# Moving the o tiles of batches 4 to 7 one slot later in a linear-attention plus MLP kernel

## Chip, cores and metric

One NeuronCore of one Trainium2 chip at a time. The metric is device time in microseconds (us), lower is better. The kernel before takes 292.99 us, the median of three runs (292.66 to 293.11). The experiments were run in three sets, each on another chip and each with the kernel before in it; ratios are taken within a set. A profile is one execution; its span is about 1.8 us shorter than the timed run.

## The reference, cut to what matters

Eight batches, eight heads, 576 rows, head width 64. Attention without a softmax, an RMS norm per head, then a residual MLP of width 512 → 2048 → 512.

```python
kv  = einsum('bhsd,bhse->bhde', k, v)          # 64 x 64 per head
out = einsum('bhsd,bhde->bhse', q, kv)         # called o below
x   = out / rms(out) * g_norm                  # 512 wide: 8 heads side by side
xn  = (x - mean(x)) / std(x) * g_ln
y   = x + relu(xn @ w_ch1) @ w_ch2
```

## The kernel before

The MLP is the bulk of the work: per batch 64 matmuls of 128x512 in `mm1` (the centred x, times `w1`) and 64 in `mm2` (times `w2`). The attention part of a batch is threaded into the MLP of earlier batches. The author does it by hand: `mm1` and `mm2` call `tick()` before every four such matmuls, and each tick is a slot, in which the work that `at(slot, ...)` put there is emitted. A slot lasts four matmuls. Batch `b` has its `mm1` in slots 32b to 32b+15 and its `mm2` in 32b+16 to 32b+31 (for b from 3 up).

```python
    def turn_q_dma(b):                  # q copied to another layout, then transposed by DMA
        q_p = kv_in.tile([128, JJ, H, D], bf16, tag="qp", bufs=2)
        nc.vector.tensor_copy(q_p.rearrange("p j h d -> p h j d"), q_in[b % NB])
        q_t = qt_pool.tile([128, JJ, HP, 128], bf16, tag="qt", name="qt")
        nc.sync.dma_start_transpose(
            q_t.rearrange("p j hp t -> p (j hp) t"), q_p.rearrange("p j h d -> p (j h d)"))
        qts[b] = q_t
    # [...]
    def plan_tile(s, make, turn_at, on_pe):
        # [...]
        def first():                    # o matmuls (PE), square (ScalarE), reduction (VectorE)
            t = make(); box.append(t); t.o(); t.sq(); t.red()
        def second():                   # 1/rms, times g_norm, centred (VectorE)
            t = box[0]; t.y(); t.x(); t.xc()
        # third: variance (ScalarE); fourth: xc transposed to xT, by DMA or on PE
        at(s, first)
        at(s + 2, second)
        at(s + 6, third)
        at(turn_at, fourth)
    # [...]
    for b in range(3, B):
        s = 32 * b
        at(47 if b == 3 else s - 60,
           lambda b=b: load_batch(b, qts[b - 1][:1, J, HP - 1, 127:]))
        d = -41 if b == 3 else -45
        at(s + d, lambda b=b: kv_of(b))
        at(s + d + 1.7, lambda b=b: turn_q_dma(b))
        for j in range(J):              # J = 4 main tiles of 128 rows
            o = s + d + (10 if b == 3 else 12) + 5 * j
            plan_tile(o, lambda b=b, j=j: main_tile(b, j), o + 6, False)
        if b % 2:                       # one remainder tile for two batches, 64 rows of each
            plan_tile(s - 14, lambda b=b: rem_tile(b), s - 8, False)
        at(s + 14, lambda b=b: rstd_of(b))
```

`turn_q_dma(b)` and `plan_tile` meet at `qt`: the o matmuls of batch b load it as their stationary operand. The second argument of `load_batch` is a gate: the loads of batch b start when `qt` of batch b-1 has landed. All DMA transposes and, but for half of those of the very last tile, all output transfers are issued by SyncE, in the order in which they are emitted.

Of the kernel before, what the change touches and what calls it, by code (L numbers as in the profile page):

```python
# [14 lines left out]
def kernel(  # L15
# [80 lines left out]
    def load_batch(b, after=None):  # L96
        if after is not None:
            nc.gpsimd.tensor_copy(gate, after)  # L98
        load(k_in[b % NB], k, b)
        load(v_in[b % NB], v, b)  # L100
        load(q_in[b % NB], q, b)
# [97 lines left out]
    def turn_q_dma(b):  # L199
# [6 lines that stand above are left out]
# [22 lines left out]
    def kv_of(b):  # L228
        kv_ps = ps_m.tile([128, HP, D], f32, tag="misc", name="kv_ps")
        kvp = held[b] = kv_pack[b % 4]  # L230
        for hp in range(HP):
            for j in range(JJ):
                for hh in range(2):
                    h = 2 * hp + hh
                    nc.tensor.matmul(kv_ps[hh * D:hh * D + D, hp, :],  # L235
                                     lhsT=k_in[b % NB][:, h, j, :], rhs=v_in[b % NB][:, h, j, :],
                                     start=(j == 0), stop=(j == JJ - 1))
        nc.scalar.copy(kvp[:D, :, :D], kv_ps[:D])  # L238
        nc.scalar.copy(kvp[D:, :, D:], kv_ps[D:])
# [104 lines left out]
    def main_tile(b, j, pool=None, tag="ops"):  # L344
        q_t, kvp = qts[b], held[b]
        if b not in blks:
            blks[b] = new_block("main", 3)
        return Tile([(slice(0, 128), lambda hp: q_t[:, j, hp, :], kvp)], blks[b], j, pool, tag)

    def rem_tile(b):  # L350
        mms = []
        for half, bb in enumerate((b - 1, b)):
            qt, kp = qts.pop(bb), held.pop(bb)
            mms.append((slice(half * 64, (half + 1) * 64),
                        lambda hp, qt=qt: qt[:, J, hp, :64], kp))
        if "rem" not in blks:
            blks["rem"] = new_block("rem", 1)
        return Tile(mms, blks["rem"], b // 2)

    def plan_tile(s, make, turn_at, on_pe):  # L360
        box = []

        def first():
            t = make()
            box.append(t)
            t.o()
            t.sq()
            t.red()

        def second():  # L370
            t = box[0]
            t.y()
            t.x()
            t.xc()

        def third():
            box[0].var()

        def fourth():
            box[0].turn(on_pe)  # L380
# [5 lines that stand above are left out]
# [22 lines left out]
    def rstd_of(b):  # L408
        rstd = work.tile([128, 4], f32, tag="rstd", bufs=3, name="rstd")
        nc.scalar.activation(rstd, blks[b][1][:, 2, :], func=AF.Sqrt, scale=1.0 / Dm, bias=eps_sb)  # L410
        nc.vector.reciprocal(rstd, rstd)  # L411
        rstds[b] = rstd
# [45 lines left out]
    def at(slot, fn):  # L458
        agenda.setdefault(int(slot), []).append((slot, fn))
# [153 lines left out]
# [5 lines that stand above are left out]
        at(s + d, lambda b=b: kv_of(b))  # L618
        at(s + d + 1.7, lambda b=b: turn_q_dma(b))
        for j in range(J):  # L620
            o = s + d + (10 if b == 3 else 12) + 5 * j
            plan_tile(o, lambda b=b, j=j: main_tile(b, j), o + 6, False)
        if b % 2:
            plan_tile(s - 14, lambda b=b: rem_tile(b), s - 8, False)
        at(s + 14, lambda b=b: rstd_of(b))
# [58 lines left out]
```

## Time and profile before

| | before |
|---|---|
| time, median of 3 | 292.99 us |
| PE busy | 97% of the span |
| waits of PE after 110 us, as PE's own row shows them | none |
| weight loads of o waiting for `qt` | 2.0 us in 4 waits |

In the views PE is TensorE, PEld its weight loads, DVE VectorE, ACT ScalarE, POOL GpSimd and SPq SyncE's queue. First the page's lines of busy time (us, share of the span, number of instructions):

```profile
span 291.4 us, 5801 instructions
PE 283.4 (97%) x2320; PEld 159.1 (55%) x2320; DVE 150.7 (52%) x335; ACT 154.7 (53%) x341; POOL 41.9 (14%) x68
```

PE is the limit, but 97% alone would not say whether matmuls run at their pace or stand waiting inside a "busy" record. The chain of waits says more. This is the chain of the kernel before around batch 5 (start in us, duration in us, what); L418 is `mm2`, L402 is `mm1`, L235 is kv and L260 is o:

```profile
131.81 0.75 PE kv_ps L235 x40
132.57 4.34 PE p L418 x20
136.91 6.20 DMA qt<-q_p
143.11 0.05 issue
143.16 0.40 PE o_ps L260 x4
143.56 0.86 PE p L418 x4
144.42 3.45 PE p L402 x16
147.87 0.22 PE o_ps L260 x4
```

Four matmuls take 0.86 us, 0.216 us each. The page "TensorE: Matmul & The Clock Gate" of the Trainium skill (section "Wait — 56ns, not 53.3ns?") gives 215.7 ns from start to start for 512 columns at full clock; the trace agrees, so these matmuls run at the pace that the page gives. The o matmuls at 143.16 take 0.40 us, those at 147.87 take 0.22. The first set waited for the `qt` transpose, which SyncE issued at 136.91 and which landed at 143.11. PE's own wait table does not list it, because the last matmuls before it are still counted as busy; the weight loads (PEld), which run ahead, show it. Their waits between 100 and 240 us:

```profile
PEld L260 <- DMA qt<-q_p: 2.0, 4, 0.6
```

For batches 4, 5, 6 and 7 the four stretches from the start of kv to the start of the `mm1` that follows hold exactly the same matmuls before and after the change (40 of kv, 52 of `mm2`, four of o). The columns are the stretch, its length, the busy time of PE, PEld, VectorE, ScalarE and GpSimd (with the number of instructions), the granted clock, the busy share of the DMA engines and their GB/s:

```profile
102.18:114.74 12.56, 12.47 (x97) 5.99 (x98) 7.56 (x17) 3.15 (x8) 0.85 (x2) 1.00 0.48 96
131.81:144.42 12.61, 12.49 (x98) 5.96 (x98) 4.42 (x9) 2.14 (x5) 0.85 (x3) 1.00 0.71 126
161.94:174.25 12.31, 12.31 (x98) 6.00 (x98) 7.01 (x14) 3.15 (x8) 0.86 (x3) 1.00 0.58 117
191.32:203.78 12.46, 12.46 (x97) 5.98 (x98) 4.41 (x9) 2.14 (x5) 0.00 (x0) 1.00 0.73 122
```

They differ by up to 0.30 us, though they hold the same work. (The 97 or 98 counted on PE are these 96 and the one or two that overlap an edge of the stretch.) The difference is put down to the wait for `qt`.

Why `qt` is late shows in SyncE's queue before the q transpose of batch 5 (start, time on the queue, line, operation):

```profile
135.51 1.29 SPq L341 DMA_TRANSPOSE xT_blk<-xc  x1
136.91 3.09 SPq L203 DMA_TRANSPOSE qt<-q_p  x1
```

The copy of q was done at 135.06 by VectorE's timeline, but the transpose of `xT` for tile 3 of batch 4 stood in front. Batch 7 is like this. In batches 4 and 6 VectorE was late instead: there the remainder tile's normalisation (from 105.08 and 164.55 us) precedes the copy of q, which ended at 108.43 and 167.92, and `qt` went out right after it, at 108.50 and 168.06.

### The profile page before, as it was taken

The numbers are of one execution on the slowest core, as the hardware profiler recorded it, in microseconds if no ns is written. First come the engines' busy times: TensorE is split into PE (matmuls) and PEld (weight loads), VectorE is DVE, ScalarE is ACT, GpSimd is POOL, SyncE is SP. The second block draws the span as 40 slices with busy tenths as digits, with TensorE's granted clock in tenths as the row PEclk, the third lists the DMA queues.
The fourth block names the chain that finished last, engine by engine and source line by source line (L and its number), as shares of the span: only waits on it lengthen the run. The fifth ranks groups of instructions, "written<-read, shape, count | busy, mean of one in ns | idle before, by whom it ended". The sixth has DMA issues, their size and how long they took to land.

```text
span 291.4 us, 5801 instructions
## 1 busy us (share of the span) xinstructions
PE 283.4 (97%) x2320; PEld 159.1 (55%) x2320; DVE 150.7 (52%) x335; ACT 154.7 (53%) x341; POOL 41.9 (14%) x68
## 2 busy tenths in 40 slices
PE   8889999999999999999999999999999999999995
PEld 3579755995578654444444444444444444444444
DVE  5776028836996893765266936752678200220022
ACT  3457755885569931882189408920894066016500
POOL 8522520032050003200220023000000000000000
PEclk9999999999999999999999999999999999999999
DMA  7999999469789818993999279939202510131033
GB/s 212 202 206 205 198 204 217 102 100 192 144 141 201 110 41 153 217 162 65 159 192 140 56 145 192 165 64 167 58 18 55 109 36 0 38 78 30 0 74 72
DMA packets 63290, 35.84 MB, mean 123 GB/s; under 512 B 30748, under 2 KB 58268, under 8 KB 63264
## 3 DMA queue, kind: packets, MB, share of 16 engines
q0 software_dynamic: 28016, 17.76, 43.8%
q1 hardware_dynamic: 34736, 16.99, 29.7%
q10 hardware_dynamic: 512, 0.72, 0.8%
q8 instruction: 18, 0.29, 0.4%
q14 instruction: 8, 0.07, 0.1%
HBM read 36.71 MB, written 9.44 MB: 158 GB/s over the span
## 4 chain that ended last, share of the span: by engine, by line
PE 83%; DMA 6%; DVE 6%; ACT 2%; issue 1%; POOL 1%; POOLq 0%
PE p L402 40%; PE p L418 36%; DMA qt<-q_p 4%; PE o_ps L260 3%; DMA q_in<-in_q_dram 2%; PE kv_ps L235 2%; DVE ss L287 1%; DVE x_blk L311 1%; DVE y L292 1%; DVE o_sb L423 1%; PE tp L183 1%; ACT m L405 1%; PE p L196 1%; ACT xT_blk L339 1%; PE tp L337 0%
## 5 line engine op out<-in xcount | busy, mean ns | idle before, releaser
L402 PE MATMUL p<-xT_blk,w_sb 128*128 128x128 bf16 (+2 forms) x1024 | 132.0, 286 | 0.5 <-ACT m L405 0.3
L418 PE MATMUL p<-w_sb,m 128*128 128x512 bf16 (+2 forms) x608 | 130.2, 368 | 0.0
L405 ACT ACTIVATE m<-p 128x512 bf16<-128x512 f32 x144 | 85.2, 597 | 45.3 <-PE p L402 43.5
L402 PEld LDWEIGHTS <-w_sb 128*128 128x128 bf16 x1024 | 78.6, 98 | 45.5 <-issue 1.1
L418 PEld LDWEIGHTS <-m 128*128 128x128 bf16 x608 | 56.6, 98 | 60.3
L423 DVE SCALAR_TENSOR_TENSOR o_sb<-p,rstd,x_blk 128x512 f32<-128x512 f32 (+2 forms) x38 | 27.3, 719 | 44.2 <-PE p L418 41.5
L266 ACT ACTIVATE sq<-o_ps 128x512 f32<-128x512 f32 x34 | 20.2, 595 | 38.9 <-PE o_ps L260 38.9
L287 DVE TENSOR_REDUCE ss<-sq 128x8 f32<-128x512 f32 x34 | 23.2, 682 | 19.8 <-ACT sq L266 19.8
L329 ACT ACTIVATE dev<-x_blk,st_blk 128x512 f32<-128x512 f32 x36 | 25.8, 718 | 6.2 <-DVE st_blk L315 6.1
L321 DVE SCALAR_TENSOR_TENSOR xc<-x_blk,st_blk,g_ln_sb 128x512 bf16<-128x512 f32 x34 | 25.6, 752 | 1.2
L292 DVE TENSOR_TENSOR y<-o_ps,inv 128x512 f32<-128x512 f32 x34 | 23.5, 691 | 2.6
L311 DVE SCALAR_TENSOR_TENSOR x_blk<-y,g_norm_sb 128x512 f32<-128x512 f32 x34 | 23.5, 691 | 1.2
L411 DVE RECIPROCAL rstd<-rstd 128x4 f32<-128x4 f32 x9 | 1.6, 174 | 39.3 <-ACT rstd L410 39.3
L304 DVE RECIPROCAL inv<-rms 128x8 f32<-128x8 f32 x36 | 7.2, 200 | 22.5 <-ACT rms L297 22.4
L98 POOL COPY gate<-qt 1x1 bf16<-1x1 bf16 x5 | 1.4, 287 | 115.3 <-DMA qt<-q_p 115.3
L297 ACT ACTIVATE rms<-ss,eps_sb 128x8 f32<-128x8 f32 x36 | 10.8, 300 | 7.8 <-DVE ss L287 7.1
L260 PEld LDWEIGHTS <-qt 128*128 128x128 bf16 (+1 forms) x152 | 9.7, 100 | 8.4 <-DMA qt<-q_p 2.0
L260 PE MATMUL o_ps<-kv_pack,qt 128*128 128x128 bf16 (+1 forms) x152 | 13.3, 221 | 0.4 <-DVE qt L191 0.2
L196 PE MATMUL p<-fill_sb 128*128 128x512 bf16 x28 | 8.6, 465 | 1.2 <-DVE eps_sb L137 1.2
L339 ACT COPY xT_blk<-tp 128x512 bf16<-128x512 bf16 x10 | 5.8, 579 | 2.3 <-PE tp L337 2.3
L329 ACT ACTIVATION_READ_ACCUMULATOR dev<-x_blk,st_blk 128x1 f32 x36 | 7.0, 193 | 0.0
L238 ACT CAST kv_pack<-kv_ps 64x256 bf16<-64x256 f32 x7 | 2.6, 365 | 7.9 <-PE kv_ps L235 7.8
(79 smaller groups left out, 119.0 us busy)
## 6 DMA issues: line engine op xcount, KB each, us to landing
out_dram<-o_sb SPq DMA_DIRECT2D x70, 128.0 KB, 2.5
w_sb<-in_moe_w_ch_dram POOLq DMA_DIRECT2D x8, 512.0 KB, 13.8
k_in<-in_k_dram POOLq DMA_DIRECT2D x7, 320.0 KB, 5.1
v_in<-in_v_dram POOLq DMA_DIRECT2D x7, 320.0 KB, 8.8
q_in<-in_q_dram POOLq DMA_DIRECT2D x7, 320.0 KB, 12.1
q_in<-in_q_dram POOLq DMA_DIRECT2D x8, 256.0 KB, 12.4
k_in<-in_k_dram POOLq DMA_DIRECT2D x7, 256.0 KB, 6.5
v_in<-in_v_dram POOLq DMA_DIRECT2D x7, 256.0 KB, 11.0
```

The costliest lines, as they stand in the source:

```text
L196: nc.tensor.matmul(p1, lhsT=fill_sb[:, :128], rhs=fill_sb, start=True, stop=True)
L260: nc.tensor.matmul(flat[rows, hp * 128:(hp + 1) * 128], lhsT=lhsT_of(hp), rhs=kvp[:, hp, :], start=True, stop=True)
L266: nc.scalar.activation(self.sq_t, self.o_ps, func=AF.Square)
L287: nc.vector.tensor_reduce(self.ss, self.sq_t, axis=AX.X, op=ALU.add)
L292: nc.vector.tensor_mul(self.y_t, self.o_ps, self.inv().to_broadcast([128, H, D]))
L311: nc.vector.scalar_tensor_tensor(x_blk[:, ts].rearrange("p (h d) -> p h d", h=H), in0=self.y_t, scalar=1.0, in1=g_norm_sb.to_broadcast([12 ...
L321: nc.vector.scalar_tensor_tensor(self.xc_t, in0=x_blk[:, self.ts], scalar=st[:, 1, self.ts:self.ts + 1], in1=g_ln_sb, op0=ALU.add, op1=ALU ...
L329: nc.scalar.activation(dev, x_blk[:, ts], func=AF.Square, bias=st[:, 1, ts:ts + 1], accum_out=st[:, 2, ts:ts + 1])
L402: nc.tensor.matmul(p1[:, i, :], lhsT=w1_sb[:, kk, de * 128:(de + 1) * 128], rhs=blk[2][:, kk, sl], start=(kk == 0), stop=(kk == nK - 1))
L405: nc.scalar.activation(m1[:, de0:de0 + per, sl], p1, func=AF.Relu)
L418: nc.tensor.matmul(p2[:, c0:c1], lhsT=m1s[b][:, de, ts * 128:(ts + 1) * 128], rhs=w2_sb[:, de, c0:c1], start=(de == 0), stop=(de == nDe - 1))
L423: nc.vector.scalar_tensor_tensor(o_sb[:, c0:c1], in0=p2[:, c0:c1], scalar=rstds[b][:, ts:ts + 1], in1=blks[b][0][:, ts, c0:c1], op0=ALU.mu ...
```

## The change

Its intent is to let the first o tile of a batch ask for `qt` one slot (0.86 us) later, when it has landed. The work and the resources are the same; the o matmuls of all four tiles of batches 4 to 7 and everything that hangs on them move one slot. The number that changes, 12 or 13, is called the offset below.

```diff
-            o = s + d + (10 if b == 3 else 12) + 5 * j
+            o = s + d + (10 if b == 3 else 13) + 5 * j
```

Two orders that matter change with it, as a comparison of the emitted instructions shows. On PE the first o tile now stands before the first matmul of `mm1` instead of four matmuls earlier. On SyncE the q transpose of batches 5, 6 and 7 now stands ahead of the `xT` transpose of tile 3 of the batch before, which moved from slot 116 (for batch 4) to 117, while the q transpose stays at 116.7.

## The prediction

> What bounds the kernel now: TensorE (PE). The page gives PE 97% busy; in the wait table PE's waits sum to under 4 us, all in the first 30 us. Busy time alone proves little, so I checked the rate: in the chain of waits 64 matmuls of 128x512 take 13.81 us, 215.8 ns each. The Trainium skill (TensorE: Matmul & The Clock Gate, section "Wait — 56ns, not 53.3ns?") gives 215.7 ns start to start for a warm array; the trace agrees. So from 115 us on PE streams at its limit, except at one place per batch: the first o tile of the next batch. There the waits of the weight loads (PEld) show "L260 <- DMA qt<-q_p", 0.58, 0.61, 0.31 and 0.48 us for batches 4, 5, 6, 7 (at 113.5, 143.1, 173.0, 202.5 us). Part is hidden under the matmul still running: from the end of kv to the start of mm1 the chain has 11.81, 11.85, 11.56, 11.71 us, against 52 x 0.2158 + 0.22 = 11.44 us without a wait. PE loses 0.37 + 0.41 + 0.12 + 0.27 = 1.17 us.
>
> What the change does. Nothing is added or removed. The o matmuls of the four tiles of batches 4 to 7, with square, reduction, normalisation, variance and transposing DMA, move one slot (four matmuls, 0.86 us) later; kv and the q transpose stay.
> 1. The first o tile asks for qt 0.86 us later, in mm1's first slot. That covers all four waits (longest 0.61 us): up to -1.17 us.
> 2. In SyncE's order the qt transpose of batches 5, 6, 7 now precedes the xT transpose of tile 3 of the batch before (the instruction order shows the swap). That xT held back qt of batches 5 and 7 (issued at 136.9 and 196.4 us): they should go out about 1.5 us earlier. The loads gated by qt start earlier too.
> 3. xT of tile 3 now follows qt's 3.03 us issue. Batch 3 shows this order already: qt issued 108.50, xT 111.58, landed 2.5 us later. For batches 4 and 6 it lands near 141 and 200.5 us, needed at 144 and 203.5: harmless. For batch 5 the remainder tile keeps VectorE busy until the q copy: qt went out at 168.06, and with tile 3's chain a slot later about 0.4 us after that. xT goes out near 171.6 and lands near 174.1, where mm1 of batch 5 wants it at about 174.0. I expect a new PE wait of 0 to 0.5 us, about 0.2. Batch 7 has no qt behind it.
> 4. ScalarE gets four squares and two variances per mm1 stretch instead of three and three: as full as before. VectorE is 52% busy. No PE wait from either.
>
> Sum: -1.17 + 0.2, about -1.0 us, all on the critical path.
>
> Prediction: 292.0 us, 8 in 10 between 291.3 and 292.9. Faster by over 2%: 0.005; within 2%: 0.99; slower by over 2%: 0.005.
>
> What would show each step: (1) no L260 wait on qt after 110 us. (2) qt issue of batches 5 and 7 about 1.5 us earlier relative to their kv. (3) A PE wait at the start of mm1 of batch 5 only, 0 to 0.5 us. (4) No PE wait on relu (L405) after 110 us; 64 matmuls still 13.81 us.
>
> What would make it wrong: xT of tile 3 landing late because the earlier loads collide with it (transposes issued during loads took 7 to 9 us to land, at 119.2, 124.1, 178.7 us), which could hold mm1 by some us; relu late because the square now stands ahead of mm1's first relu; or variation between runs, as large as the effect.

## The result, and the profile after

The changed kernel took 292.28 us, the median of four runs (292.10 to 292.49), against 293.01 for the kernel before. The ratio is 0.9978, with a 95% interval of 0.9960 to 0.9995. A ratio is the mean time of one kernel's fast runs over that of the other's of the same rounds, so it is not quite the ratio of the medians. A second set of five rounds on another occasion gave 292.12 us and a ratio of 0.9972 (0.9959 to 0.9985). The gain is 0.7 to 0.8 us by the medians, a quarter of one per cent, and clear of noise.

The page after:

```profile
span 290.4 us, 5803 instructions
PE 282.2 (97%) x2320; PEld 159.3 (55%) x2320; DVE 150.8 (52%) x335; ACT 155.5 (54%) x341; POOL 41.1 (14%) x68
```

The chain of the changed kernel around batch 5:

```profile
131.26 0.75 PE kv_ps L235 x40
132.02 11.33 PE p L418 x52
143.34 0.22 PE o_ps L260 x4
143.57 4.32 PE p L402 x20
```

No DMA is left in it. The o matmuls take 0.22 us, as everywhere. The weight loads have no wait for `qt` at all between 100 and 240 us. The four stretches after:

```profile
101.89:114.19 12.30, 12.30 (x97) 6.07 (x98) 7.61 (x17) 2.55 (x7) 0.54 (x2) 1.00 0.47 93
131.26:143.57 12.31, 12.31 (x98) 6.08 (x98) 4.78 (x9) 1.54 (x4) 1.38 (x3) 1.00 0.72 129
161.09:173.40 12.31, 12.31 (x98) 6.07 (x98) 7.18 (x16) 2.55 (x7) 0.90 (x3) 1.00 0.49 97
190.47:202.77 12.30, 12.30 (x97) 6.07 (x98) 4.77 (x9) 1.55 (x4) 0.00 (x0) 1.00 0.73 121
```

They are equal to 0.01 us and sum to 49.22 us, 0.72 us less than before. From the start of kv of batch 4 to the last output operation on VectorE the chain takes 185.00 us, before it took 185.72 (287.90 - 102.18): the same 0.72 us, so nothing else after 102 us changed. The spans of the two profiles differ by 1.0 us; the other 0.3 us lie ahead of 102 us, in the loading stage, which the change does not touch.

SyncE's queue at the q transpose of batch 5, after:

```profile
135.01 3.17 SPq L203 DMA_TRANSPOSE qt<-q_p  x1
138.23 1.28 SPq L341 DMA_TRANSPOSE xT_blk<-xc  x1
```

The swap is there. From the start of kv, `qt` goes out after 3.75 us (135.01 - 131.26) where it took 5.10, and for batch 7 after 3.75 where it took 5.09.

### The profile page after: what moved, and what is told of

Its sections match the earlier page's. It is cut to its first block, busy times and chain, and to the rows that moved or that the text cites. A ratio compares the mean times of both kernels' runs of the same rounds, so it can differ in the third digit from the quotient of the medians.

```text
span 290.4 us, 5803 instructions
## 1 busy us (share of the span) xinstructions
PE 282.2 (97%) x2320; PEld 159.3 (55%) x2320; DVE 150.8 (52%) x335; ACT 155.5 (54%) x341; POOL 41.1 (14%) x68
## 4 chain that ended last, share of the span: by engine, by line
PE 85%; DVE 5%; DMA 4%; ACT 2%; issue 1%; POOL 1%; SPq 0%; DVEq 0%; POOLq 0%
PE p L402 40%; PE p L418 38%; DMA q_in<-in_q_dram 2%; PE o_ps L260 2%; DMA out_dram<-o_sb 2%; PE kv_ps L235 2%; DVE o_sb L423 1%; DVE ss L287 1%; ACT m L405 1%; DVE x_blk L311 1%; DVE y L292 1%; PE tp L183 1%; PE p L196 1%; DVE xc L321 1%; ACT sq L266 0%
## 5 line engine op out<-in xcount | busy, mean ns | idle before, releaser
L196 PE MATMUL p<-fill_sb 128*128 128x512 bf16 x28 | 8.0, 437 | 1.2 <-DVE eps_sb L137 1.2
```

The source lines that it names most:

```text
L196: nc.tensor.matmul(p1, lhsT=fill_sb[:, :128], rhs=fill_sb, start=True, stop=True)
```

## The experiments

So the gain could have come from three things that the change does at once. Theory W: the first o tile no longer waits for `qt`. Rival B: the ScalarE and VectorE work of all four tiles falls into a better place. Rival S: the swap on SyncE does it. Two measures are given for each run: the four stretches (exact, but of one execution) and the ratio to the kernel before (five rounds, and four runs for the first result). The median of the kernel before was 292.92, 292.93 and 292.86 us in the three sets of runs.

| run | time, us | ratio (95%) | four stretches, us | kv of batch 4 to last output, us |
|---|---|---|---|---|
| before | 292.99 | 1 | 49.94 | 185.72 |
| after | 292.28 | 0.9978 (0.9960–0.9995) | 49.22 | 185.00 |
| after_again | 292.12 | 0.9972 (0.9959–0.9985) | 49.22 | 185.01 |
| first_tile_only | 292.22 | 0.9976 (0.9964–0.9988) | 49.29 | 185.00 |
| rest_only | 293.02 | 1.0012 (0.9996–1.0027) | 49.63 | 185.44 |
| xT_after_qt_only | 292.61 | 0.9998 (0.9985–1.0011) | 49.67 | 185.46 |
| early_q | 292.34 | 0.9984 (0.9972–0.9996) | 49.22 | 185.00 |
| o_at_11 | 296.17 | 1.0110 (1.0097–1.0123) | 53.44 | 189.22 |
| o_at_14 | 292.64 | 0.9987 (0.9970–1.0004) | other work in them | 185.45 |
| o_at_16 | 299.65 | 1.0232 (1.0207–1.0257) | other work in them | 193.31 |
| rem_beside_kv | 291.74 | 0.9962 (0.9950–0.9973) | 48.99 | 184.67 |
| rem_beside_kv_all | 291.95 | 0.9960 (0.9943–0.9978) | 48.97 | 184.66 |
| kv_in_two | 293.50 | 1.0016 (0.9999–1.0033) | 50.12 | 185.91 |

All gave correct results. The edits from first_tile_only to o_at_14 are shown against the kernel before, those of the last three (rem_beside_kv, rem_beside_kv_all, kv_in_two) against the changed kernel; that of rem_beside_kv_all comes on top of rem_beside_kv's.

### after_again

The changed kernel itself, once more.

> The changed kernel again, for a tighter interval: 0.7 us under the kernel before (ratio 0.9976), four stretches 49.2 us.

Measured: 292.12 us, 49.22 us in the stretches. The trace repeats to 0.01 us.

### first_tile_only

```diff
-            o = s + d + (10 if b == 3 else 12) + 5 * j
+            o = s + d + (10 if b == 3 else (13 if j == 0 else 12)) + 5 * j
```

> Only tile 0 of batches 4 to 7 moves one slot later; tiles 1 to 3 and the order of the SyncE queue stay. Measure: the sum of the four stretches from the start of kv to the start of mm1 (batches 4 to 7), 49.94 us in the kernel before and 49.22 in the changed one. Theory W (all the gain is the four waits of the first o tile for the q transpose): the whole gain, 49.2 us, about 292.3 us. Rival B (the gain comes from ScalarE and VectorE work of all four tiles falling better into mm1): about a quarter, 49.75 us, 292.8 us. Rival S (it comes from the q transpose going ahead of the xT transpose on SyncE): nothing, 49.9 us, 293.0 us.

Measured: 292.22 us; 185.00 us from kv of batch 4 to the last output, the same as the changed kernel, and no wait for `qt`. (Its 49.29 contains 0.07 us by which one kv stretch of this trace starts earlier because of a lost record.) SyncE's order here is the old one: `xT` goes out at 134.96 us and `qt` of batch 5 behind it at 136.35. One tile in four has the whole gain, without the swap: this speaks against B, and it shows that S is not needed.

### rest_only

```diff
-            o = s + d + (10 if b == 3 else 12) + 5 * j
-            plan_tile(o, lambda b=b, j=j: main_tile(b, j), o + 6, False)
+            o = s + d + (10 if b == 3 else (12 if j == 0 else 13)) + 5 * j
+            plan_tile(o, lambda b=b, j=j: main_tile(b, j), o + (5 if b > 3 and j > 0 else 6), False)
```

> Only tiles 1 to 3 of batches 4 to 7 move one slot later; their transposing DMAs are asked for in the old slots, so the SyncE order is the old one. Theory W: nothing, 49.9 us in the four stretches and 293.0 us. Rival B: about three quarters, 49.4 us, 292.5 us. Rival S: nothing.

Measured: 293.02 us, a ratio of 1.0012: no gain, so B falls. (One of its six executions took 294.32 us with a granted clock of 0.994; the other five, at 0.997 or more, took 292.62 to 293.17.) The one trace is not as clean as expected: 49.63 instead of 49.9. Batches 4 and 7 waited as before (12.58 and 12.42 us), batch 5 hardly (12.33 instead of 12.61), although `qt` went out 5.09 us after kv, as before. So a single wait varies by about 0.3 us, presumably with the time that the transpose takes to land (the trace has no landing for this one), and "0.72 us" is the value of one execution, and only the rounds say what the mean is.

### xT_after_qt_only

```diff
-            plan_tile(o, lambda b=b, j=j: main_tile(b, j), o + 6, False)
+            plan_tile(o, lambda b=b, j=j: main_tile(b, j), o + (7 if b > 3 and j == 3 else 6), False)
```

> No tile moves; only the xT transpose of tile 3 is asked for one slot later, so that the q transpose goes ahead of it. Theory W: the q transposes of batches 5 and 7 go out about 1.5 us earlier and their waits (0.30 and 0.16 us) go, those of batch 4 (0.26 us) and 6 (0.01 us) stay: 49.5 us in the four stretches, 292.5 us. Rival B: nothing, 49.9 us. Rival S: the whole gain, 49.2 us, 292.3 us.

Measured: in the trace the swap does what W says for the two batches that it concerns: the stretches of batches 5 and 7 are 12.31 and 12.30 us. Batch 4 keeps its wait (12.59), and batch 6 has one here too (12.47): its `qt` landed 5.0 us after issue instead of 4.9. The median, 292.61 us, is near the expected 292.5, but the ratio, 0.9998 (0.9985 to 1.0011), leaves a gain of this size open. It is pulled up by one execution of six, 293.94 us with a granted clock of 0.994; the other five took 292.58 to 292.70, 0.2 to 0.3 us under the median of the kernel before (292.92). S is refuted as the whole cause, because the waits of batches 4 and 6 remain in the trace.

### early_q

```diff
-        at(s + d + 1.7, lambda b=b: turn_q_dma(b))
+        at(s + d + (1.7 if b == 3 else 0.7), lambda b=b: turn_q_dma(b))
```

> No tile moves; the q copy and q transpose of batches 4 to 7 are asked for one slot earlier, so qt should land 1 to 3 us earlier in all four batches. Theory W: the whole gain without moving a tile, 49.2 us in the four stretches, 292.3 us, no wait for qt left. Rival B: nothing, 49.9 us, 293.0 us. Rival S: the whole gain too, since the q transpose is ahead of xT here as well.

Measured: 292.34 us, and in the trace exactly the changed kernel: stretches of 12.30, 12.31, 12.31 and 12.30 us. (This execution was 0.4 us later already at kv of batch 4, 102.28 us against 101.89, before the edit acts.) `qt` went out 2.2 to 3.1 us after kv instead of 5.1 to 6.3. Two different ways to make `qt` ready before it is asked for end at the same length. S expects this too; W is settled by this run and first_tile_only together.

### o_at_11

```diff
-            o = s + d + (10 if b == 3 else 12) + 5 * j
-            plan_tile(o, lambda b=b, j=j: main_tile(b, j), o + 6, False)
+            o = s + d + (10 if b == 3 else 11) + 5 * j
+            plan_tile(o, lambda b=b, j=j: main_tile(b, j), o + (6 if b == 3 else 7), False)
```

> The opposite of the change: the o tiles of batches 4 to 7 one slot earlier than in the kernel before (slot offset 11 in place of 12), their xT transposes in the old slots, SyncE order as before. Theory W: each first tile asks for qt 0.86 us earlier, and qt comes when it came: 4 x 0.86 = 3.45 us more waiting, four stretches 53.4 us, about 296.4 us. Rival B: a loss like the gain, about 0.7 us, 50.7 us and 293.7 us.

Measured: 296.17 us, 53.44 us in the stretches. The opposite of the change costs 3.5 us in the trace, 3.2 us by the medians, where the change gave 0.7. With waits this long PE's own table (PE, 100 to 240 us) sees most of them:

```profile
PE o_ps L260 <- DMA qt<-q_p: 3.5, 4, 1.3
```

So the same step of 0.86 us per batch has a value of 3.5 us on one side and 0.7 us on the other (both from the traces): only the part of the step up to the landing of `qt` counts.

### o_at_16

```diff
-            o = s + d + (10 if b == 3 else 12) + 5 * j
+            o = s + d + (10 if b == 3 else 16) + 5 * j
```

> The o tiles four slots later than in the kernel before (offset 16, the latest that the kernel allows). Theory W: no more to gain past the first slot, since no wait for qt is left. The other side of the bargain should show: xT of tile 3 now goes out behind the q transpose and two output transfers, for batch 5 near 171.3 us on the clock of the changed kernel's trace, landing 2.5 us later near 173.8, while mm1 of batch 5 wants it at 173.4: a PE wait of 0.3 to 0.6 us there, none for batch 4, 0 to 0.3 us for batch 6. So 0.3 to 0.9 us slower than the changed kernel, 292.6 to 293.2 us. If xT had no such limit: 292.3 us.

Measured: 299.65 us, 7.5 us over the changed kernel where I had expected 0.3 to 0.9. The direction was right, the size was not. PE waits for `xT` of tile 3 in three batches, 5.4 us in total, and once 0.4 us for VectorE's output operation. The end of the chain before `mm1` of batch 5 (the copy of q on VectorE, the q transpose and two output transfers on SyncE's queue, then `xT`):

```profile
169.91 0.83 DVE q_p L201
170.88 3.10 SPq L203
174.07 0.55 SPq L436
174.67 0.59 SPq L437
175.31 2.56 DMA xT_blk<-xc
177.91 4.15 PE p L402 x12
```

I had put the late transposes on the clock of the changed kernel, with `qt` issued at 167.0. But at offset 16 the normalisations of tile 3 and of the remainder tile stand together on VectorE, ahead of the copy of q, and hold it back; `qt` goes out at 170.88, and two output transfers and then `xT` follow it in SyncE's order. In batches 4 and 6, too, tile 3's chain now precedes the copy of q.

The last line has a second loss in it: 12 matmuls take 4.15 us instead of 2.6 (12 x 0.216). PE stood for 2.9 us, from 175.04 to 177.91, and the granted clock fell meanwhile (columns as above; the number after POOL's is the clock):

```profile
177.00:178.00 1.00, 0.09 (x1) 0.09 (x2) 0.00 (x0) 0.00 (x0) 1.00 (x3) 0.68 0.72 55
178.00:179.00 1.00, 1.00 (x3) 0.35 (x4) 0.00 (x0) 0.00 (x0) 1.00 (x2) 0.50 0.38 31
```

Up to 177 us the clock was 1.00, and from 181 us on it is again. A mean of 0.68 over one microsecond is 0.64 us at half clock, so that it fell near 177.36, when PE had stood for 2.3 us. The slow clock adds about 1.5 us to a wait of 2.9. This execution took 300.54 us, and it is one of three out of six with a granted clock of 0.993 or 0.994 (300.32 to 301.10 us); the other three, at 0.998 or more, took 298.69 to 298.99 us. The page "TensorE: Matmul & The Clock Gate" (section "What's actually happening") says that the array falls to half clock after an idle window of about 3.4 us and comes back after a busy one. The fall and the return agree; the idle time that sufficed here was shorter, 2.3 us.

### o_at_14

```diff
-            o = s + d + (10 if b == 3 else 12) + 5 * j
+            o = s + d + (10 if b == 3 else 14) + 5 * j
```

> The o tiles two slots later than in the kernel before, one later than in the changed one. Theory W: no wait for qt is left to remove, and the q copy is not yet delayed, so the same as the changed kernel: no PE wait after 110 us, 292.2 us. If the late xT of the offset 16 began here already: a wait of L402 for xT at batch 5, some tenths of a us.

Measured: 292.64 us; 185.45 us from kv of batch 4 to the last output, 0.45 us over the changed kernel. The plateau that I expected does not exist, and the other outcome that I had named appeared, at two places rather than one. PE's chain of this kernel at the start of `mm1` of batches 3 and 5:

```profile
113.87 1.02 PE p L402 x4
...
173.29 1.04 PE p L402 x4
```

Each set of four takes 0.16 to 0.18 us more than 0.86, and an idle piece of 0.03 to 0.05 us stands before it. At batch 5 the weight loads name `xT` as what they waited for (0.5 us). At batch 3 they name no releaser, but `xT` of its tile 3 landed at 113.6 (issued 111.12, 2.5 us), just when it was wanted. In the changed kernel the o tile of the next batch stands directly before that first `mm1` matmul and gives `xT` another 0.22 us; at offset 14 it stands four matmuls behind. So `xT` and not only `qt` bounds the place from the other side, and offset 13 fits between the two with little room.

### rem_beside_kv

The changed kernel still has equal stretches of 12.30 us where 40 kv matmuls (0.75 us), 52 x 0.2158 us and 0.22 us of o would be 12.19. Each of those stretches has a spell of matmuls of half width (64 columns of the array, kv and the remainder tile's o), and the time after such a spell is 0.11 us too long. The page "TensorEngine Tiling (Array Packing)" of the Trainium skill (section "Key Properties") says: "Mode switching requires drain". To try whether each change of width costs time, two such spells were put side by side.

```diff
-            plan_tile(s - 14, lambda b=b: rem_tile(b), s - 8, False)
+            plan_tile(s - 13, lambda b=b: rem_tile(b), s - 7, False)
```

> The changed kernel with the remainder tile of batches 3, 5 and 7 one slot later, so that for batches 3 and 5 its half-width o matmuls stand directly before the half-width kv matmuls. In the trace of the changed kernel each spell of half-width matmuls is followed by 0.11 us more than 0.216 us per matmul accounts for (four matmuls in 0.97 us, 52 in 11.33 us). If that is a cost of each spell, two spells fewer save 2 x 0.11 = 0.22 us, or up to 0.44 us if going in costs as much as coming out: 292.0 us. If it is something else: 292.3 us.

Measured: 291.74 us and a ratio of 0.9962, against 292.12 us and 0.9972 for the changed kernel in the same rounds: 0.3 to 0.4 us less, the fastest median of all kernels here. The intervals of the two ratios overlap, so this rests on the trace. The chain of the changed kernel around the remainder tile and kv of batch 4:

```profile
98.62 0.22 PE o_ps L260 x4
98.85 1.73 PE p L418 x8
100.57 0.34 PE o_ps L260 x8
100.92 0.97 PE p L418 x4
101.89 0.75 PE kv_ps L235 x40
102.64 11.33 PE p L418 x52
113.97 0.22 PE o_ps L260 x4
```

And of this one:

```profile
98.62 0.22 PE o_ps L260 x4
98.84 2.59 PE p L418 x12
101.43 0.34 PE o_ps L260 x8
101.77 0.63 PE kv_ps L235 x40
102.41 11.33 PE p L418 x52
113.73 0.22 PE o_ps L260 x4
```

The same 64 `mm2` matmuls, 8 of the remainder tile and 40 of kv end 0.24 us earlier. Four `mm2` matmuls after the remainder tile no longer take 0.97 us, and kv takes 0.63 us instead of 0.75 when half-width matmuls precede it: about 0.11 us to leave a spell and 0.12 us to enter one. The runs show this cost, and not that a drain is its cause: the first weight load of a spell starts only with its matmul (both at 100.50 us in the changed kernel), and a load that could not run ahead would look the same. From 98.62 us to the last output it is 187.82 us instead of 188.27, twice 0.23, as the upper end of the expectation had it. (The table's last column starts at kv of batch 4, when 0.12 us of this are already saved.)

### rem_beside_kv_all

```diff
-    plan_tile(62, lambda: rem_tile(1), 69, False)
+    plan_tile(55, lambda: rem_tile(1), 62, False)
```

> As the kernel with the remainder tile beside kv, and the remainder tile of batch 1 moved 7 slots earlier to stand before kv of batch 3 too: one spell fewer, 0.23 us less than that kernel, about 291.5 us, unless VectorE (the busiest stretch of the kernel, 70 to 90 us) falls behind from it and PE waits there for a relu or an xT.

Measured: 291.95 us, no better than rem_beside_kv. After 98.95 us the trace is the same length (187.82 us to the last output). Ahead of it PE has a new wait of 0.3 us, for VectorE to free the buffer of an o tile (o_ps after y). The expectation had feared a wait there, for a relu or an `xT`. That the spell was saved and then given back in this way is read from one trace, not tested; between 67 and 87 us the chain runs mostly over VectorE in both kernels, so that PE time saved ahead of it need not count.

### kv_in_two

```diff
-        at(s + d, lambda b=b: kv_of(b))
+        at(s + d, lambda b=b: kv_of(b, 0, HP // 2))
+        at(s + d + 1, lambda b=b: kv_of(b, HP // 2, HP))
```

(`kv_of` cut so that it does the head pairs from one number to another; the copies to `kv_pack` after the second half.)

> The changed kernel with the kv matmuls of batches 3 to 7 in two halves, in two slots one after the other, so that there are five half-width spells more and not one matmul more. If a spell costs 0.23 us of PE time (what taking two away saved, each), the four stretches grow from 49.22 to 50.14 us and the run by 5 x 0.23 = 1.15 us, to about 293.3 us. If the 0.11 us had another cause than the change of width: no change, 292.2 us.

Measured: 293.50 us, 1.4 us over the changed kernel's 292.12 by the medians, which come from two sets of rounds; by the ratios of the two sets to the kernel before (1.0016 and 0.9972) it is 1.3 us. Its chain at batch 5:

```profile
131.67 0.43 PE kv_ps L239 x20
132.10 0.97 PE p L424 x4
133.07 0.43 PE kv_ps L239 x20
133.51 10.47 PE p L424 x48
143.97 0.22 PE o_ps L266 x4
144.20 4.32 PE p L408 x20
```

From kv to `mm1` it is 12.53 us (144.20 - 131.67), 0.22 to 0.23 more than 12.31 with not one matmul more; the four stretches sum to 50.12 us, where 50.14 were expected. Each spell costs 0.23 us of PE time, shown from both sides. The run itself grew by 0.1 to 0.2 us more than five spells account for; where that lies was not looked for.

## Why the prediction was right or wrong, point by point

The predicted 292.0 us (291.3 to 292.9) holds the measured 292.28. The sign, the class and the place of the effect were right. The sum came out at -0.7 instead of -1.0 us, and two terms of it were off, in opposite directions: 0.44 us too much gain and 0.2 us of a loss that did not come. That they cancel in part is luck. The range, 1.6 us wide, is twice as wide as the effect, so that the hit alone says little; the mechanism rests on the experiments.

- What bounds the kernel: right. PE runs at 0.216 us per matmul from about 110 us on, and the only loss that the change could reach was the wait for `qt`.
- Point 1, the waits go: right, and shown by taking them away in two other ways (first_tile_only, early_q) and by making them longer (o_at_11). The size was off. I took 11.44 us as the length from the end of kv to `mm1` without a wait, computed as 52 x 0.2158 + 0.22. This is the term that was mis-sized. In the changed kernel, without any wait, it is 11.55 us in all four batches (for batch 5, 143.57 - 132.02). The missing 0.11 us is the passage from half-width to full-width matmuls after kv, as rem_beside_kv and kv_in_two showed later. Four times 0.11 is 0.44, so that the "1.17 us" were 0.73 us of waiting (0.26 + 0.30 + 0.01 + 0.16) and 0.44 us of this passage, which no shift of o tiles removes. The undisturbed batch 6 in the trace before already stood at 11.56; I booked 0.12 us of wait for it and should have asked why the best case missed the arithmetic.
- Point 2, the swap and the earlier `qt`: right, 1.35 us earlier for batches 5 and 7 instead of 1.5. It was not needed for the gain (first_tile_only has none of it); alone it removes two of the four waits in the trace (xT_after_qt_only).
- Point 3, a new wait for `xT` at batch 5 of about 0.2 us: it did not come, which lies inside the 0 to 0.5 that I gave. I expected `qt` of batch 6 to go out 0.4 us later relative to kv. It went out 0.18 us earlier (167.03 - 161.09 = 5.94 us after kv; before, 168.06 - 161.94 = 6.12). In the new ScalarE order the variance of tile 3 stands behind the square root for the remainder tile and no longer ahead of it; the remainder tile's normalisation starts 2.43 us after kv instead of 2.61. That this order is the reason was read from order and trace, not tested. `xT` then went out at 170.15; it took 2.5 us to land and was there near 172.7, and `mm1` began at 173.40. But the worry was sound: at one slot later (o_at_14) the wait of 0.2 us is there, and at three later (o_at_16) it dominates.
- Point 4, no trouble from ScalarE or VectorE: right. PE has no wait for a relu after 110 us, and 64 matmuls of `mm1` still take 13.81 us. rest_only shows no gain from the shift of the other three tiles by itself.
- The risk that earlier loads would delay `xT`: for batch 6 it took 3.9 us to land instead of 2.5, and there was still room (landed at 201.43, `mm1` at 202.77).

## What to carry to other kernels

When an engine is near full, take its loss from the distance between two fixed points of its program, and take the undisturbed length from an occurrence that has no wait, not from multiplying matmul durations: here the arithmetic was 0.11 us short at each place and blew a gain of 0.73 us up to 1.17. A shift of a consumer is worth only the wait that it covers, and it pulls its own products later: look up what the moved work must still deliver, in this case `xT`, and how little room that has, before shifting further "to be safe". Putting matmuls of the same array tiling next to each other is worth 0.23 us for each spell saved here, a third of what this change brought.

## What the Trainium skill lacked or had wrong

- "TensorEngine Tiling (Array Packing)", section "Key Properties", says that a switch of tiling mode drains TensorE, and gives no figure there. No run here shows the drain itself, but a spell of half-width matmuls cost 0.23 us: about 0.12 us to enter and 0.11 us to leave (kv 0.63 instead of 0.75 us; four `mm2` matmuls 0.97 instead of 0.86 us; kv in two halves 12.53 instead of 12.31 us).
- "TensorE: Matmul & The Clock Gate", section "What's actually happening", ties the fall to half clock to an idle window of about 3.4 us. In o_at_16 PE stood for 2.9 us, and the clock fell after 2.3 us of it (0.68 in the microsecond around its end, 0.50 in the next); 12 matmuls then took 4.15 us instead of 2.6. It is one wait in one trace.
- "DMA: Bandwidth & Descriptors", section "Latency and other measured facts", gives a bandwidth for DMA transposes, and not how long one takes from issue to landing. Here, on SyncE: the q transpose 4.9 to 6.9 us from issue (3.0 to 3.3 us of it on the queue), an `xT` transpose directly behind it 2.5 to 4.0 us, and 7 to 9 us for those of the kernel before that were issued at 119.17, 124.05 and 178.66 us, while loads were running.
